# A row buffer that outlives its stage, and final stores cut into parts

## The chip, the cores and the metric

The kernel runs on one core of a Trainium2 chip. The metric is the device time of one launch in microseconds (us), shown as the median of several runs. Beside it stands one profiled execution, whose span, from the first to the last instruction, is a little shorter than the time of the same run. Engines: PE (TensorE), DVE (VectorE), ACT (ScalarE), POOL (GpSimd) and SP (SyncE, which here only issues DMAs).

## The reference

```python
# attention with random features, per batch (8) and head (8); q, k, v: 576 x 64; omega: 128 x 64
phi(x) = exp(h - max(h)) / sqrt(128),  h = x @ omega.T - |x|^2 / 2,  x scaled by 64**-0.25
attn   = (phi(q) @ (phi(k).T @ v)) / (phi(q) @ sum(phi(k)) + 1e-6)
x      = attn as (8, 576, 512)
# Fourier mixing, a norm and an MLP
u   = x + real(fft(fft(x, axis=1), axis=2))
un  = (u - mean(u)) / sqrt(var(u) + 1e-6)
out = u + relu(un @ w_ch1) @ w_ch2        # 512 -> 2048 -> 512, on 4608 rows
```

All is in 32-bit floats; the two MLP weights come in as 64-bit and are converted on the chip.

## The kernel before

The program has two parts. The first computes attention and mixing for all batches, writes `u` to a scratch tensor `us` in device memory, converts the weights, and already runs the MLP for the first 4 tiles of 128 rows (the "plain" blocks, `plain_of`, lines 862 to 923). The second part runs the MLP for the other 4096 rows in 8 blocks (`NTB`) of 512 rows, numbered j.

**The plain blocks.** Each multiplies by `w1` (L894), applies relu into `ht`, and multiplies by `w2` (L917) into a PSUM bank. `rest` (L925) loads the rows of `u` into a buffer `ur`, adds the bank (L930), and `store_rows` (L808) issues two stores of 64 rows (L810). `ur` is a tile with one buffer in the pool `mlpp`. This pool, `fix`, `ld`, `att` and `fft` are closed together by `early.close()` (L1066). The pool `late` (L1076) is opened after that and takes their room. Before all of them lie `const` and `slabs`, which live through both parts.

**A block of the second part.** Both matrix products use Strassen-like schemes of seven products.

- `first_of(j, fc)` (L1087) makes the hidden layer, for 8 values of `fc`. Its matmuls are L1099, each of the seven products 4 matmul records in the trace. Partial results are copied from PSUM into `s` by ACT (L1113) and added by DVE into `hid` (L1085); POOL forms sums `hs` (L1166). The weight sums `w1s` for groups 1 to 3 are written by DVE (L1045) at the start of the second part.
- `product_of(j, i, cells)` (L1193) makes one of seven products `i`, in the order 1, 2, 4, 5, 6, 7, 3 (`ORDER`), against weights that were prepared in device memory as `w2l`. Each product is split again into seven leaves (L1252, 8 matmul records each), which use operands loaded into a ring of tiles `wl` (L1182, `NWL` = 14 buffers, 256 KB a load), issued on SP's queue. The leaves run in the order 1, 2, 5, 6, 3, 7, 4. DVE adds bank and saved copy into quarters of `part` (c11, c12, c22; L1232); after the last leaf, ACT copies the fourth quarter, c21, from PSUM (L1282). `plus` (L1285) then adds `part` to a "cell" (L1289), on DVE or POOL.
- `second_of(j, cells)` (L1314) loads the rows of `u` of the block into two cells (tile `ur2`, each 128 partitions x 2 sets of 128 rows x 512 columns, shown as `ur` in the trace), and when all products that go into a cell are done it stores them, with four DMAs of 64 rows on SP (`stored`, L1322). A cell has a left and a right half of 256 columns (`HM`). The left half of cell 0 needs products 1 and 2; its right half needs 6, 5 and, last of all, 3. Cell 1 needs 4, 5, 6 and 7.

**What sets the order.** The order of the instructions on each engine is written by `Listing` (L82), a small planner that runs while the program is built: every piece of work is a `Step` with an engine, an assumed duration, the events and buffers that it waits for, and a bias; the step with the lowest sum of earliest begin and bias comes next, and takes its place on its engine. `port` marks steps of which only one may run on DVE and POOL together in the plan. The chip then runs each engine's list in order, with waits. SP's DMAs too are issued strictly in list order: a store that waits for its data holds up the loads behind it.

Of the kernel before, what the change touches and what calls it, by code (L numbers as in the profile page):

```python
# [14 lines left out]
ALU = mybir.AluOpType  # L15
AX = mybir.AxisListType
F32 = mybir.dt.float32
# [16 lines left out]
PE, ACT, DVE, POOL, SP, NONE = "pe", "act", "dve", "pool", "sp", "none"  # L34
# [192 lines left out]
def kernel(  # L227
# [10 lines left out]
    nc = tc.nc  # L238
# [3 lines left out]
    DM = H * D  # L242
# [10 lines left out]
    P = 128  # L253
# [9 lines left out]
    TP = 128  # L263
    NPLAIN = 4
    TB = 512
    NWL, NSUM = 14, 3
    NTB = (B * S - NPLAIN * TP) // TB
    HF, HT, HM = NFC // 2, TB // 2, DM // 2
    D2, F2 = NDC // 2, DFF // 2
# [6 lines left out]
    const = ctx.enter_context(tc.tile_pool(name="const", bufs=1))  # L276
# [2 lines left out]
    w1 = const.tile([128, NDC, DFF], F32, name="w1")  # L279

    slabs = ctx.enter_context(tc.tile_pool(name="slabs", bufs=4))
    ident = const.tile([128, 128], F32, name="ident")
    mhalf = const.tile([P, 1], F32, name="mhalf")

# [5 lines left out]
    mlpp = early.enter_context(tc.tile_pool(name="mlp", bufs=2))  # L290
# [495 lines left out]
    def rows_of(t):  # L786

        b, n = tiles[t]
        for i in range(2):
            h = slice(64 * i, 64 * i + 64)  # L790
            c, r = (b, n + i) if n else (b + i, 0)
            u0 = 64 * (n - 1 + i) if n else 2 * NL * P
            rows = out[c].rearrange("(p r) d -> r p d", r=R)[r]
            ev = ("us", c) if n > 4 else ("us", c, n // 2 if n else NL, 0)
            yield h, us[c][u0 : u0 + 64, :], rows, ev
# [4 lines left out]
    def load_rows(dst, t):  # L800
        b, n = tiles[t]
        if n:
            nc.sync.dma_start(dst, us[b][64 * (n - 1) : 64 * (n + 1), :])
        else:
            for h, u, _, _ in rows_of(t):
                nc.sync.dma_start(dst[h], u)

    def store_rows(t, src):  # L808
        for h, _, rows, _ in rows_of(t):
            nc.sync.dma_start(rows, src[h])  # L810

    unTs = {}

# [48 lines left out]
    def plain_of(j):  # L862
# [39 lines left out]
        for i in range(nt):  # L902
            for f0 in range(0, NFC, 2):
                yield Step(
                    PE,
                    1.72,
                    after=tuple(("ht", key, f) for f in (f0, f0 + 1))
                    + tuple(("w", NDC * DFF // CV + f) for f in (f0, f0 + 1)),
                    take=("bank",) if f0 == 0 else (),
                    give=("ht", "ht") if i == nt - 1 else (),  # L910
                    makes=("op", nt * j + i) if f0 == NFC - 2 else None, bias=0.24,
                )
                if f0 == 0:
                    b, yp = got()
                    yield Fork(rest(nt * j + i, b, yp))
                for fc in range(f0, f0 + 2):
                    nc.tensor.matmul(  # L917
                        yp[:, 0:DM],
                        lhsT=hs[fc][:, 128 * i : 128 * i + 128],
                        rhs=w2[:, fc, :],  # L920
                        start=(fc == 0),
                        stop=(fc == NFC - 1),
                    )

    def rest(t, b, yp):  # L925
        yield Step(SP, 0.5, 2.7, take=("ur",), kb=256)
        ur = mlpp.tile([P, DM], F32, name="ur", tag="ur", bufs=1)
        load_rows(ur[:], t)
        yield Step(DVE, 0.7, after=(("op", t),), give=(b,), bias=1.38)
        nc.vector.tensor_tensor(out=ur[:], in0=ur[:], in1=yp, op=ALU.add)  # L930
        yield Step(SP, 0.4, 2.5, give=("ur",), kb=256)
        store_rows(t, ur[:])
# [238 lines left out]
    ORDER = (1, 2, 4, 5, 6, 7, 3)  # L1171
# [13 lines left out]
    def factor(i):  # L1185

        g, t0 = {1: (0, 0), 2: (HF, 0), 4: (HF, HT), 7: (0, HT)}.get(i, (None, 0))
        if g is None:
            n = {5: 0, 6: 1, 3: 2}[i]
            return lambda t, f: hs[:, 4 * f : 4 * f + 4, n, 128 * t : 128 * t + 128]  # L1190
        return lambda t, f: hid[:, g + 4 * f : g + 4 * f + 4, t0 + 128 * t : t0 + 128 * t + 128]

    def product_of(j, i, cells):  # L1193
        a = factor(i)
        me = ("second", j, i)
        name = {1: "c11", 2: "c21", 4: "c22"}.get(i)

        def ready(*fq):
            fs = [f for q in fq for f in range(4 * q, 4 * q + 4)]
            return tuple((("first", j, f), name) if name else ("hs", j, f) for f in fs)  # L1200
# [3 lines left out]
        part = late.tile([128, 2, HM], F32, name="part", tag="part", bufs=4)  # L1204
# [34 lines left out]
        def leaf(n, ps, left, start, after=(), give=(), take=(), makes=None):  # L1239
            yield Step(  # L1240
                PE,
                0.895,
                after=(("wl", j, i, n),) + after,
                take=take,
                give=("wl",) + give,
                makes=makes, bias=0.3,
            )
            b = None
            if take:
                b, ps = got()  # L1250
            for f in range(4):
                nc.tensor.matmul(  # L1252
                    ps[:, 0:128],
                    lhsT=left[:, f],
                    rhs=wls[j, i, n][:, f],
                    start=start and f == 0,
                    stop=(f == 3),
                    skip_group_check=True,
                )
            return b, ps  # L1260

        def of_sum(n):
# [3 lines left out]
        xb, x = yield from leaf(1, None, a(0, 0), True, ready(0), take=one)  # L1266
# [11 lines left out]
        yield from leaf(  # L1278
            4, x, a(1, 1), False, ((me, "c22"),), give=("set", "sums"), makes=(me, "read")
        )  # L1280
        yield Step(ACT, 0.26, 0.1, give=(xb,), makes=(me, "c21"))
        nc.scalar.activation(out=part[:, 1, 0:128], in_=x[:, 0:128], func=AF.Copy)  # L1282
        yield Step(NONE, after=tuple((me, c) for c in ("c11", "c12", "c22")))
# [10 lines left out]
        def done(n):  # L1294
            return (("second", j, n), "done")

        us = tuple(("ur2", j, t) for t in range(2))
        if i in (1, 6, 7):
            if i != 1:
                before = {6: 1, 7: 6}[i]  # L1300
                yield from plus(cells["u"][:], part[:], after=(done(before),), give=("part",))
            to = {1: ((0, 0),), 6: ((0, 1),), 7: ((1, 1), (1, 0))}[i]
            part, give = cells["u"], ("part",) if i == 7 else ()
        else:
            to = {2: ((0, 0),), 4: ((1, 0),), 5: ((0, 1), (1, 1)), 3: ((0, 1),)}[i]
            give = ("part",)
        for n, (t, m) in enumerate(to):
# [3 lines left out]
                makes=done(i) if last else None,  # L1311
            )

    def second_of(j, cells):  # L1314
        t0 = (NPLAIN * TP + TB * j) // 128
        for t in range(2):
            yield Step(SP, 0.9, 3.0, take=("ur",), kb=512, makes=("ur2", j, t))
            cells[t] = late.tile([P, 2, DM], F32, name="ur2", tag="ur2", bufs=3)
            for n in range(2):
                load_rows(cells[t][:, n], t0 + 2 * t + n)  # L1320

        def stored(t, *after):  # L1322
            yield Step(
                SP, 0.9, 2.5, give=("ur",), after=tuple((("second", j, i), "done") for i in after),
                kb=512,
            )
            for n in range(2):
                store_rows(t0 + 2 * t + n, cells[t][:, n])

        yield Fork(stored(1, 4, 5, 7))  # L1330
        yield Fork(stored(0, 1, 2, 3, 5, 6))

        yield Step(
            NONE, after=tuple((("second", j, i), "read") for i in ORDER[:-1]), give=("ht",) * NFC
        )

    def halves():
        for j in range(NTB):
            for fc in range(HF):
                yield Step(NONE, take=("set", "ht", "ht"))  # L1340
                yield Fork(first_of(j, fc))
            cells = {}
            yield Fork(second_of(j, cells))
            for i in ORDER:
                yield Step(NONE, take=("set",))
                yield Fork(product_of(j, i, cells))
# [36 lines left out]
```

## Time and profile before

| | us |
|---|---|
| median of 3 runs | 1234.14 |
| lowest, highest | 1232.59, 1235.41 |
| profiled run: time | 1233.62 |
| profiled run: span | 1231.7 |
| second part, from its first matmul | about 468.5 to the end |
| last matmul's end | 1224.4 |

The profile's first part gives the busy time of each engine; its chain follows back from the last instruction to what released it, step by step. Beside the page, the trace answers questions: who waited for whom in a stretch of time, the chain in order of time, the busy time and granted TensorE clock of short stretches, and single instructions in order of time (start, duration, engine, line, what is written and read, how often, and in brackets how long the engine stood idle before and what released it). "SPq" stands for a DMA issued by SP, and its duration is the time that issuing takes; when the data has landed is told apart.

### The profile page before, as it was taken

The numbers are of one execution on the slowest core, as the hardware profiler recorded it, in microseconds if no ns is written. First come the engines' busy times: TensorE is split into PE (matmuls) and PEld (weight loads), VectorE is DVE, ScalarE is ACT, GpSimd is POOL, SyncE is SP. The second block draws the span as 40 slices with busy tenths as digits, with TensorE's granted clock in tenths as the row PEclk, the third lists the DMA queues.
The fourth block names the chain that finished last, engine by engine and source line by source line (L and its number), as shares of the span: only waits on it lengthen the run. The fifth ranks groups of instructions, "written<-read, shape, count | busy, mean of one in ns | idle before, by whom it ended". The sixth has DMA issues, their size and how long they took to land.

```text
span 1231.7 us, 31634 instructions
## 1 busy us (share of the span) xinstructions
PE 1192.3 (97%) x12705; PEld 1067.8 (87%) x12705; DVE 745.0 (60%) x1519; ACT 458.9 (37%) x1434; POOL 384.8 (31%) x451
## 2 busy tenths in 40 slices
PE   7889899999999999999999999999999999999997
PEld 6777878878878786899899899899899899899897
DVE  3888899887677643285185175276266266267255
ACT  6867768676664321222222222222222222222211
POOL 2353534532012012422431432431521431431421
PEclk9999999999999999999999999999999999999999
DMA  9564655636654324096186186276277277268255
GB/s 255 159 185 147 190 169 169 209 105 203 179 191 157 126 90 163 9 306 183 34 286 194 43 273 195 54 256 200 59 245 218 60 232 231 60 205 258 60 176 158
DMA packets 148737, 206.00 MB, mean 167 GB/s; under 512 B 49264, under 2 KB 62320, under 8 KB 148592
## 3 DMA queue, kind: packets, MB, share of 16 engines
q1 hardware_dynamic: 143984, 187.22, 49.4%
q0 software_dynamic: 4608, 16.78, 4.2%
q8 instruction: 100, 1.64, 0.5%
q14 instruction: 45, 0.37, 0.1%
HBM read 172.23 MB, written 35.91 MB: 169 GB/s over the span
## 4 chain that ended last, share of the span: by engine, by line
PE 91%; DVE 4%; ACT 2%; issue 1%; DMA 1%; SPq 0%; DVEq 0%; ACTq 0%
PE banks L1099 31%; PE banks L1252 29%; PE banks L515 5%; PE banks L917 5%; PE banks L894 4%; PE banks L441 4%; PE banks L683 4%; PE banks L549 3%; PE banks L592 2%; PE banks L710 2%; DVE nmx L459 2%; ACT e L476 1%; PE banks L833 1%; PE banks L715 1%; DVE raw L387 1%
## 5 line engine op out<-in xcount | busy, mean ns | idle before, releaser
L1085 DVE CUSTOM_DVE_ANT_0 hid<-banks,s 128x256 f32<-128x256 f32 x192 | 79.8, 423 | 256.3 <-PE banks L1099 256.3
L1252 PE MATMUL banks<-wl,sums 128*128 128x128 f32 x1792 | 220.3, 275 | 0.0
L1252 PEld LDWEIGHTS banks<-wl,sums 128*128 128x128 f32 x1792 | 210.5, 192 | 1.0
L476 ACT ACTIVATE e<-banks,nmx 128x128 f32<-128x128 f32 x576 | 160.1, 394 | 36.9 <-DVE nmx L459 36.8
L1113 ACT ACTIVATE s<-banks 128x256 f32<-128x256 f32 x192 | 73.4, 383 | 260.6 <-PE banks L1099 247.0
L1099 PE MATMUL banks<-unT,w 128*128 128x256 f32 x704 | 167.3, 379 | 0.0
L1099 PEld LDWEIGHTS banks<-unT,w 128*128 128x128 f32 x704 | 132.7, 190 | 17.9 <-issue 0.5
L1227 ACT ACTIVATE s<-banks 128x128 f32<-128x128 f32 x168 | 46.6, 277 | 236.5 <-PE banks L1252 174.6
L1099 PE MATMUL banks<-tt,w1s 128*128 128x256 f32 x512 | 127.4, 381 | 2.7 <-ACT s L1113 2.7
L459 DVE TENSOR_REDUCE nmx<-banks 128x8 f32<-128x1024 f32 (+1 forms) x96 | 88.3, 952 | 41.3 <-PE banks L515 36.7
L1099 PEld LDWEIGHTS banks<-tt,w1s 128*128 128x128 f32 x512 | 97.6, 191 | 16.4 <-ACT s L1113 3.1
L1166 POOL TENSOR_TENSOR hs<-hid 128x256 f32<-128x256 f32 x64 | 46.5, 726 | 202.7 <-DVE hid L1085 175.1
L1252 PE MATMUL banks<-wl,hid 128*128 128x128 f32 x768 | 98.8, 275 | 0.0
L1252 PEld LDWEIGHTS banks<-wl,hid 128*128 128x128 f32 x768 | 94.0, 192 | 1.2
L1232 DVE TENSOR_TENSOR part<-banks,s 128x128 f32<-128x128 f32 x168 | 48.6, 289 | 75.2 <-PE banks L1252 74.1
L1166 POOL TENSOR_TENSOR hs<-hid,hs 128x256 f32<-128x256 f32 x64 | 46.4, 726 | 118.5 <-issue 94.4
L515 PE MATMUL banks<-om,kqT 64*64 64x128 f32 x2304 | 78.0, 280 | 4.4 <-ACT kqT L448 3.0
L1099 PE MATMUL banks<-unT,w1s 128*128 128x256 f32 x320 | 81.5, 382 | 0.0
L827 POOL TENSOR_TENSOR rstd<-rstd,mhalf 128x1 f32<-128x1 f32 x36 | 29.8, 828 | 163.0 <-DVE rstd L825 163.0
L515 PEld LDWEIGHTS banks<-om,kqT 64*64 64x64 f32 x2304 | 65.2, 137 | 15.8 <-issue 4.7
L1252 PE MATMUL banks<-wl,hs 128*128 128x128 f32 x576 | 74.9, 275 | 0.4 <-DVE part L1232 0.4
L391 POOL TENSOR_TENSOR w<-w,raw 128x512 f32<-128x512 f32 x32 | 44.6, 1395 | 94.7 <-DVE raw L389 81.3
(110 smaller groups left out, 1997.0 us busy)
## 6 DMA issues: line engine op xcount, KB each, us to landing
wl<-w2l SPq DMA_DIRECT2D x392, 256.0 KB, 3.7
raw<-in_moe_w_ch_dram POOLq DMA_DIRECT2D x32, 512.0 KB, 5.2
kq<-in_k_dram SPq DMA_DIRECT2D x32, 288.0 KB, 3.7
kq<-in_q_dram SPq DMA_DIRECT2D x32, 288.0 KB, 4.1
vd<-in_v_dram SPq DMA_DIRECT2D x32, 288.0 KB, 4.7
out_dram<-ur SPq DMA_DIRECT2D x72, 128.0 KB, 2.4
u<-us SPq DMA_DIRECT2D x32, 256.0 KB, 4.2
ur<-us SPq DMA_DIRECT2D x32, 256.0 KB, 3.8
```

Of the source, the lines that this page charges most:

```text
L441: nc.tensor.transpose(ps[:, (j - j0) * 128 : (j - j0 + 1) * 128], src(j), ident[:])
L459: nc.vector.tensor_reduce(nmx[:, :, 0:num], pps[:, :, 0 : MF * num].rearrange("p b (c m) -> p b c m", m=MF), axis=AX.X, op=ALU.max, negate ...
L476: nc.scalar.activation(out=e[:, c + (i if num == 1 else 0), :], in_=pps[:, i, MF * c : MF * c + MF], func=AF.Exp, bias=nmx[:, i, c : c + 1],)
L515: nc.tensor.matmul(pps[cols, c, MF * m : MF * m + MF], lhsT=kqT[rows, j, cols], rhs=om2[rows, :],)
L683: nc.tensor.matmul(yp[:, 0:NK], lhsT=fold[:, c, n, :], rhs=tab[:, c, :], start=(c == 0), stop=(c == NC3 - 1),)
L894: nc.tensor.matmul(hp[:, 0:TP], lhsT=w1[:, dc, 128 * fc : 128 * fc + 128], rhs=unTs[key][:, dc, :], start=(dc == 0), stop=(dc == NDC - 1),)
L917: nc.tensor.matmul(yp[:, 0:DM], lhsT=hs[fc][:, 128 * i : 128 * i + 128], rhs=w2[:, fc, :], start=(fc == 0), stop=(fc == NFC - 1),)
L1085: nc.vector._custom_dve(TENSOR_ADD_SAT, out=o, in0=ps, in1=sb, s0=FMAX, s1=0.0)
L1099: nc.tensor.matmul(ps[:, 0:HT], lhsT=left(dc), rhs=right(dc), start=start and dc == 0, stop=(dc == D2 - 1), skip_group_check=True,)
L1113: nc.scalar.activation(out=s[:], in_=ps[:, 0:HT], func=AF.Copy)
L1166: nc.gpsimd.tensor_tensor(out=o, in0=l, in1=r, op=op)
L1252: nc.tensor.matmul(ps[:, 0:128], lhsT=left[:, f], rhs=wls[j, i, n][:, f], start=start and f == 0, stop=(f == 3), skip_group_check=True,)
```

## The change

There are three edits.

1. The row buffer of the plain blocks is no longer a tile of the pool `mlpp`, but a tile `ur1` of `const`, so that it keeps its place in the second part. It takes 2 KB of each partition, which the pool `late` then lacks; the ring `wl` gets 13 buffers instead of 14.
2. `store_rows` gets two more arguments, the columns to store and the queue for each half of the rows. In the last block the left half of cell 0 is stored after products 1 and 2. For the blocks before it the stores stay as they are. The assumed duration of `stored` in the planner goes from 0.9 to 2.4.
3. The last product (block 7, product 3) ends in a new function `ends`. For the first set of rows, once c11 and c12 are there, DVE adds them to the cell (128 x 256), and SP stores the right halves with two DMAs of 64 rows. For the second set of rows DVE adds c22 to the cell, and, after the last leaf, adds c21 straight from PSUM (128 x 128 each); then SP stores the first 64 rows and ACT the other 64. ACT's copy of c21 and the addition of the whole `part` to the cell are gone for this product.

```diff
-    NWL, NSUM = 14, 3
+    NWL, NSUM = 13, 3
...
     slabs = ctx.enter_context(tc.tile_pool(name="slabs", bufs=4))
+    ur1 = const.tile([128, DM], F32, name="ur1")
...
-    def store_rows(t, src):
-        for h, _, rows, _ in rows_of(t):
-            nc.sync.dma_start(rows, src[h])
+    def store_rows(t, src, cols=slice(None), queues=(nc.sync, nc.sync)):
+        for q, (h, _, rows, _) in zip(queues, rows_of(t)):
+            if q is not None:
+                q.dma_start(rows[:, cols], src[h])
...
-        ur = mlpp.tile([P, DM], F32, name="ur", tag="ur", bufs=1)
+        ur = ur1
...
+    def ends(j, me, part, x, cell):
+        t = (NPLAIN * TP + TB * j) // 128
+        before = tuple((("second", j, i), "done") for i in (5, 6))
+
+        def rows(n, e, queues, *after):
+            yield Step(e, 0.6, 2.5, after=after, kb=64)
+            store_rows(t + n, cell[:, n], slice(HM, DM), queues)
+
+        def first_rows():
+            yield Step(DVE, 0.42, after=((me, "c11"), (me, "c12")) + before, makes=(me, "r0"), port=True)
+            nc.vector.tensor_tensor(out=cell[:, 0], in0=cell[:, 0], in1=part[:, 0], op=ALU.add)
+            yield from rows(0, SP, (nc.sync, nc.sync), (me, "r0"))
+
+        yield Fork(first_rows())
+        for c, what, given in ((slice(128, 256), "c22", None), (slice(0, 128), "read", x)):
+            yield Step(DVE, 0.28, after=((me, what),) + before, makes=(me, "r1"), port=given is None)
+            nc.vector.tensor_tensor(
+                out=cell[:, 1, c],
+                in0=cell[:, 1, c],
+                in1=part[:, 1, c] if given is None else given[:, 0:128],
+                op=ALU.add,
+            )
+        yield Fork(rows(1, ACT, (None, nc.scalar), (me, "r1")))
+        yield from rows(1, SP, (nc.sync, None), (me, "r1"))
...
+        if (j, i) == (NTB - 1, ORDER[-1]):
+            yield from ends(j, me, part, x, cells[0][:, :, HM:DM])
+            return
...
-        def stored(t, *after):
+        def stored(t, cols, *after):
...
-                SP, 0.9, 2.5, give=("ur",), after=tuple((("second", j, i), "done") for i in after),
+                SP, 2.4, 2.5, give=("ur",), after=tuple((("second", j, i), "done") for i in after),
...
-                store_rows(t0 + 2 * t + n, cells[t][:, n])
-
-        yield Fork(stored(1, 4, 5, 7))
-        yield Fork(stored(0, 1, 2, 3, 5, 6))
+                store_rows(t0 + 2 * t + n, cells[t][:, n, cols], cols)
+
+        yield Fork(stored(1, slice(0, DM), 4, 5, 7))
+        if j < NTB - 1:
+            yield Fork(stored(0, slice(0, DM), 1, 2, 3, 5, 6))
+        else:
+
+            yield Fork(stored(0, slice(0, HM), 1, 2))
```

## The prediction

> **What bounds the kernel now.** I read the page first: the busy shares and the chain that ended last.
>
> ```profile
> span 1231.7 us, 31634 instructions
> PE 1192.3 (97%) x12705; PEld 1067.8 (87%) x12705; DVE 745.0 (60%) x1519; ACT 458.9 (37%) x1434; POOL 384.8 (31%) x451
> PE 91%; DVE 4%; ACT 2%; issue 1%; DMA 1%; SPq 0%; DVEq 0%; ACTq 0%
> ```
>
> TensorE (PE) is the bound almost everywhere, so a change can only pay where PE stands still or after its last matmul. Then I asked for the waits of PE alone from 460 us to the end, which is the whole second part:
>
> ```profile
> PE banks L1099 <- ACT s L1113: 2.7, 1, 2.7
> PE banks L1252 <- DVE part L1232: 0.4, 1, 0.4
> ```
>
> In 770 us PE waits twice. The long wait lies where the second part begins; the chain in order of time shows what it hangs on:
>
> ```profile
> 458.37 10.32 PE banks L917 x24
> ...
> 468.71 0.70 DVE ur L930
> ...
> 469.43 0.51 SPq L810
> ...
> 469.99 2.36 DMA out_dram<-ur
> ...
> 472.66 0.39 ACT s L1113
> 473.05 0.04 issue
> 473.09 9.08 PE banks L1099 x33
> ```
>
> The reader is to see that the first ScalarE (ACT) copy of the second part waits until the last plain block's row buffer `ur` has landed in the output; `ur` has nothing to do with `s`. The waits between 470 and 490 us name the same store for VectorE's (DVE) first write of `w1s`, another new tile, and SP's list names it for the first `wl` load. Three unrelated tiles wait for one buffer of 2 KB a partition: tiles of the pool `late` wait for everything that lived in the pools whose room they take, and `ur` is the last of it.
>
> Next, engines and clock in short stretches around the stall:
>
> ```profile
> 468.00:470.40 2.40, 2.40 (x10) 1.52 (x8) 0.69 (x1) 0.00 (x0) 0.00 (x0) 1.00 0.00 0
> 470.40:473.00 2.60, 0.00 (x0) 0.00 (x0) 0.56 (x1) 0.34 (x2) 0.00 (x0) 1.00 0.44 101
> 473.00:474.00 1.00, 0.91 (x2) 0.73 (x3) 0.97 (x3) 0.32 (x2) 0.00 (x0) 0.62 0.56 39
> 474.00:475.00 1.00, 1.00 (x4) 0.81 (x3) 1.00 (x3) 0.00 (x0) 0.00 (x0) 0.50 0.97 363
> 475.00:476.00 1.00, 1.00 (x4) 0.81 (x3) 0.96 (x3) 0.38 (x1) 0.00 (x0) 0.50 1.01 350
> 476.00:477.00 1.00, 1.00 (x4) 0.79 (x4) 1.00 (x3) 0.00 (x0) 0.00 (x0) 0.67 1.01 291
> ```
>
> The number behind the stretch is its length, then PE's busy time with its count; the third number from the end is the granted clock. The stall costs twice: PE is empty, and then runs at half clock to about 476.7 us.
>
> Last, the end of the program in order of time:
>
> ```profile
> 1222.86 0.29 DVE L1232 TENSOR_TENSOR part<-banks,s 128x128 f32<-128x128 f32 x1 [0.53 <-PE banks L1252]
> 1223.07 0.68 DVE L1289 TENSOR_TENSOR ur<-ur,part 128x512 f32<-128x512 f32 x1
> 1223.21 1.16 PE L1252 MATMUL banks<-wl,hs 128*128 128x128 f32 x8 [0.38 <-DVE part L1232]
> 1223.82 4.98 SPq L810 DMA_DIRECT2D out_dram<-ur  x8
> 1224.45 0.28 ACT L1282 ACTIVATE part<-banks 128x128 f32<-128x128 f32 x1 [3.10 <-PE banks L1252]
> 1224.77 0.69 DVE L1289 TENSOR_TENSOR ur<-ur,part 128x512 f32<-128x512 f32 x1 [1.01 <-ACT part L1282]
> ```
>
> The chain view ends at this DVE addition (1225.46), which misleads: SP issues eight stores back to back from 1223.82, four for the rows of cell 1 and four for cell 0, and is busy to 1228.80. All eight land 2.4 us after their issue, the early as the late, so they don't queue in the DMA engines; SP's issuing is the limit.
>
> [...] No ScalarE store is in this trace.
>
> **Part 1: `ur` moves into `const`.** The other last users of the early pools are the matmuls of L917 (`w2`, `ht`), over at 468.7. With `ur` gone from there, ACT's first copy needs only its own product. PE's product p1 runs 468.51 to 469.54; the copy takes 0.38 and ends near 469.95; p5 fills PE to 470.23 at its usual pace, so the next product finds its operand there. The next products, with the same copies, run from 477.48 without a wait.
>
> The saving is read from the start of the sixth product: before, it is at 477.48. A product is 4 matmul records, and 28 of them take 6.05 us at full clock (from the chain), 0.216 each. Without the stall five products from 468.51 end at 468.51 + 20 x 0.216 = 472.83. Difference 4.65 us: 2.69 of empty PE and about 1.9 of slow clock. From there PE has no wait but the 0.4 near the end, so all of it reaches the end.
>
> What could give it back: DVE's twelve weight sums (L1045) move from 472.44 to about 469.41, only 3.03 earlier, so DVE falls 1.6 us behind PE. Its three additions to `hid` end at 481.12 before, 478.09 after; the first product that needs one of them (`tt,w`) starts at 485.25 before, 480.60 after: 2.5 us to spare. SP's first `wl` load moves from 472.48 to about 470.6, behind the two stores; the first leaf needs it after 510 us. The reuse of one `ur` by four plain blocks waits for the same landings as before. Cost of these: nothing.
>
> **Part 2: ring `wl` of 13, not 14.** A load is issued when the leaf 14 places back has been read. In the last block's matmul stretch a leaf takes 0.87 us (8 records of 0.109) and a load lands in 3.3 to 4.5 us (5.5 at most in the run). With 13 it must land within 12 x 0.87 = 10.4 us. Nearly 5 us spare, and PE shows no wait for `wl` at all: nothing.
>
> **Part 3: the left half of cell 0 stored early.** Four stores after product 2, whose last addition is POOL's at 1196.42 to 1197.69. They take 4 x 0.62 = 2.5 us of SP among the `wl` loads and hold up those behind them by that, plus what SP waits for the addition (under 1 us: the written order and the addition both follow PE). Within the 5 us: nothing.
>
> **Part 4: the end.** Removed: ACT's copy (0.28), the 128x512 addition (0.69), and four of the eight closing stores. Added: `r0`, DVE 128x256; from the rows of 128 (0.29) and 512 (0.68) I interpolate 0.42 [...]; two 128x128 additions of 0.29, one reading PSUM, as L1232 already does; two stores of half rows, then one each from SP and ACT. `stored(1)` stays. The order is the listing's. Following its rule (earliest begin plus bias) with its own durations, DVE's order comes out as c22, `r0`, first `r1`, product 7's last addition, second `r1`; SP's as two stores of `r0`, four of cell 1, one of `r1`.
>
> On the clock of before: c22 at 1222.86; `r0` 1223.07 to 1223.49; first `r1` from 1223.41; product 7's addition 1223.62 to 1224.30 (0.55 later than now); second `r1` behind the last matmul, 1224.45 to 1224.74. SP: first store at 1223.56, then one per 0.627 (1223.82 to 1228.2 in seven steps); the third, cell 1's first, at 1224.81, when its data is ready; the seventh at 1223.56 + 6 x 0.627 = 1227.32. The last issue of before was at 1228.2: 0.9 us gained. ACT's store, issued near 1224.8, lands near 1227.2 and binds nothing.
> Bounds: half-row stores may be shorter (0.47 is the shortest issue of L810; three at 0.12 less) and land 0.2 sooner: gain up to 1.5, and 1.9 if `r0` comes ahead of c22. If the listing puts cell 1 first, SP starts at 1224.38 and ends its issues at 1228.14: no gain; a second queue to close may add 0.3 (estimate, like the closing steps of 0.3 each after 1230.6). I take 0.9, with -0.3 to 1.9.
>
> **Sum:** 4.65 + 0.9 = 5.55 us; span 1231.7 to 1226.15. The profiled run took 1233.62 against a span of 1231.7; the median is 1234.14. Taken from the median: 1228.6 us.
>
> **Rivals.**
> A (72%), the forecast: both parts work. 1228.6; own range 1226.3 to 1230.7. [...]
> B (13%): the stall goes, but its slow clock is not lost in the median run, or the end gives nothing: saving 2.7 to 4.65, so 1229.5 to 1231.4; I put it at 1230.5. [...] Against: the profiled run shows 0.50.
> C (8%): the change doesn't do its work at the start, because some other early buffer is released as late or new tiles wait for whole engines. Only the end gains: 1233.2. Against: ACT is released 0.01 us after the landing of `ur`'s store, and nothing else ends near.
> D (7%), slower: the ring of 13 starves PE. If a load's turn, from the freed buffer to use, reaches L, a leaf takes L/13. Up to 11.3 us (13 x 0.87) nothing happens. At 11.6, 0.023 x 392 leaves = 9 us are lost: 1228.6 + 9 = 1237.6, past 0.2% slower. For it: one leaf less of cover, and the early stores in SP's queue. Against: landings of at most 5.5 us, and no wait of PE.
>
> **How the numbers follow.** A measurement of this kernel can tell about 0.2% (2.5 us) from no change; the three times of before spread over 2.8. Faster: A and B, 85%. Same: C, 8%. Slower: D, 7%. The range leaves out C and D (15%) and a little of A's tails: 1226.2 to 1231.6.
>
> **What would show it.** Right: no PE wait on `s` near 470 us, the clock at 1.00 there, the `tt,w1s` products running on from 469.37; PE's last matmul near 1219.7; SP's last store about 2.9 us after PE's end; last ACT instruction a store. Wrong: PE idle near 470 for another releaser (C); PE or PEld waits naming `wl` (D); cell 1's stores first or SP idle between the closing stores (part 4); a PE wait on `hid` near 480 (part 1's give-back).

## The result, and the profile after

The changed kernel's median is 1228.55 us (1226.36 to 1230.91, 4 runs); its ratio to the kernel before is 0.9954, 95% interval 0.9931 to 0.9976. The forecast was 1228.6. The interval leaves out 1, so the gain is real, if small. The profiled execution of it has a span of 1228.9, more than the 1226.15 of the sum; where the difference lies is told below. The page's first lines and its chain:

```profile
span 1228.9 us, 31624 instructions
PE 91%; DVE 4%; ACT 3%; DMA 1%; issue 1%; SPq 0%; DVEq 0%; ACTq 0%
```

The waits of PE from 455 us to the end:

```profile
PE banks L1281 <- DMA wl<-w2l: 0.4, 1, 0.4
PE banks L1281 <- DVE part L1261: 0.4, 1, 0.4
```

The wait of 2.7 us is gone; a wait on the ring `wl` is new, which the prediction did not expect. (Lines have moved: L1102 is L1099 of before, L1281 is L1252, L1116 is L1113, L1261 is L1232, L1321 is L1289.) The same short stretches as before; the second part now begins at 470.46:

```profile
470.40:473.00 2.60, 2.60 (x13) 2.25 (x12) 2.31 (x4) 0.77 (x2) 0.00 (x0) 1.00 0.17 38
473.00:474.00 1.00, 1.00 (x6) 0.87 (x6) 1.00 (x3) 0.38 (x1) 0.00 (x0) 1.00 0.88 182
474.00:475.00 1.00, 1.00 (x7) 0.87 (x6) 0.96 (x2) 0.00 (x0) 0.00 (x0) 1.00 0.96 268
```

PE is busy throughout, and the clock stays at 1.00, in the later stretches up to 484 us too. The end, in order of time:

```profile
1220.81 0.29 DVE L1261 TENSOR_TENSOR part<-banks,s 128x128 f32<-128x128 f32 x1 [0.53 <-PE banks L1281]
1221.01 0.68 DVE L1321 TENSOR_TENSOR ur<-ur,part 128x512 f32<-128x512 f32 x1
1221.15 1.16 PE L1281 MATMUL banks<-wl,hs 128*128 128x128 f32 x8 [0.38 <-DVE part L1261]
1221.61 0.42 DVE L1207 TENSOR_TENSOR ur<-ur,part 128x256 f32<-128x256 f32 x1
1221.76 4.31 SPq L813 DMA_DIRECT2D out_dram<-ur  x7
1222.35 0.29 DVE L1213 TENSOR_TENSOR ur<-ur,banks 128x128 f32<-128x128 f32 x1
1222.66 0.56 ACTq L813 DMA_DIRECT2D out_dram<-ur  x1
```

SP issues seven stores instead of eight, and starts as long before PE's end (0.55 us) as it did before. In the order of DVE's additions product 7's last addition (L1321) still comes right behind c22, ahead of `r0` (L1207), so cell 1's stores are still the first.

Three stretches of an execution can be read from the timelines: up to the second part's first matmul; from there to PE's last matmul; from there to the span's end. All runs, the experiments told below included (us):

| run | first part | second part's matmuls | end | PE waits on `wl` |
|---|---|---|---|---|
| before | 468.51 | 755.86 | 7.33 | none |
| changed | 470.46 | 751.85 | 6.59 | 0.4 |
| ring 13 alone | 468.41 | 756.45 | 7.34 | 0.4 |
| `ur` in `const` alone (ring 13) | 467.85 | 751.24 | 7.31 | none |
| end alone | 471.75 | 755.81 | 6.54 | none |
| before with filler | 465.40 | 754.18 | 7.32 | none |
| changed, ring 12 | 467.31 | 761.77 | 6.62 | 6.0 |
| changed, loads in order of use | 468.08 | 751.19 | 6.53 | none |
| changed, two queues | 469.74 | 751.23 | 5.23 | none |
| changed, `r0` ahead | 466.77 | 751.20 | 5.93 | none |
| changed, three edits | 466.64 | 751.21 | 4.75 | none |
| changed, again | 469.67 | 751.21 | 6.52 | none |

The first column scatters by 6 us, though no edit changes the order of work there; the other two repeat to 0.1 us where nothing was edited, but for the wait on `wl`, which comes and goes. So a question of 1 us is put to the profile's stretches, and the timed ratios are the check.

### The profile page after: what moved, and what is told of

Its sections match the earlier page's. It is cut to its first block, busy times and chain, and to the rows that moved or that the text cites. A ratio compares the mean times of both kernels' runs of the same rounds, so it can differ in the third digit from the quotient of the medians.

```text
span 1228.9 us, 31624 instructions
## 1 busy us (share of the span) xinstructions
PE 1193.4 (97%) x12705; PEld 1068.7 (87%) x12705; DVE 745.9 (61%) x1521; ACT 458.5 (37%) x1433; POOL 385.4 (31%) x451
## 4 chain that ended last, share of the span: by engine, by line
PE 91%; DVE 4%; ACT 3%; DMA 1%; issue 1%; SPq 0%; DVEq 0%; ACTq 0%
PE banks L1102 31%; PE banks L1281 28%; PE banks L920 5%; PE banks L897 5%; PE banks L517 4%; PE banks L443 4%; PE banks L685 4%; PE banks L551 3%; PE banks L594 3%; ACT e L478 2%; PE banks L712 2%; PE banks L836 1%; DVE nmx L461 1%; PE banks L717 1%; PE banks L602 1%
## 5 line engine op out<-in xcount | busy, mean ns | idle before, releaser
L1281 PE MATMUL banks<-wl,sums 128*128 128x128 f32 x1792 | 220.2, 275 | 0.0
L1281 PEld LDWEIGHTS banks<-wl,sums 128*128 128x128 f32 x1792 | 210.5, 192 | 1.0
L1116 ACT ACTIVATE s<-banks 128x256 f32<-128x256 f32 x192 | 73.6, 383 | 255.8 <-PE banks L1102 255.8
L1102 PE MATMUL banks<-unT,w 128*128 128x256 f32 x704 | 167.3, 379 | 0.0
L1102 PEld LDWEIGHTS banks<-unT,w 128*128 128x128 f32 x704 | 132.7, 190 | 17.9 <-issue 0.5
L1102 PE MATMUL banks<-tt,w1s 128*128 128x256 f32 x512 | 126.3, 379 | 0.0
L1102 PEld LDWEIGHTS banks<-tt,w1s 128*128 128x128 f32 x512 | 97.3, 190 | 13.2
L1281 PE MATMUL banks<-wl,hid 128*128 128x128 f32 x768 | 98.9, 275 | 0.4 <-DMA wl<-w2l 0.4
L1281 PEld LDWEIGHTS banks<-wl,hid 128*128 128x128 f32 x768 | 94.0, 192 | 1.8 <-DMA wl<-w2l 0.6
L1261 DVE TENSOR_TENSOR part<-banks,s 128x128 f32<-128x128 f32 x168 | 48.6, 290 | 75.9 <-PE banks L1281 74.8
L1102 PE MATMUL banks<-unT,w1s 128*128 128x256 f32 x320 | 80.6, 379 | 0.0
L1281 PE MATMUL banks<-wl,hs 128*128 128x128 f32 x576 | 74.9, 275 | 0.4 <-DVE part L1261 0.4
```

The lines of the kernel that those rows point to most:

```text
L1102: nc.tensor.matmul(ps[:, 0:HT], lhsT=left(dc), rhs=right(dc), start=start and dc == 0, stop=(dc == D2 - 1), skip_group_check=True,)
L1116: nc.scalar.activation(out=s[:], in_=ps[:, 0:HT], func=AF.Copy)
L1281: nc.tensor.matmul(ps[:, 0:128], lhsT=left[:, f], rhs=wls[j, i, n][:, f], start=start and f == 0, stop=(f == 3), skip_group_check=True,)
```

## The experiments

**The ring alone.** Label e1_ring13.

```diff
-    NWL, NSUM = 14, 3
+    NWL, NSUM = 13, 3
```

> The kernel before with one edit: the ring wl has 13 buffers instead of 14; ur stays in the early pool and the end is as it was. My theory: a ring of 13 is at the edge, since leaves of three products are interleaved and the loads come in another order than they are used; the 15th load of a block is issued 5.4 us before its use and lands in up to 5.7 us. So 0 to 0.65 us of PE wait on wl in some of the 8 blocks, in all 0 to 2 us slower than before, and the 2.7 us stall near 470 us still there. Rival (my prediction as it was): the ring has 5 us to spare, no wait of PE on wl, ratio 1.000.

Measured: ratio 1.0006 (0.9992 to 1.002). The waits of PE from 400 us on:

```profile
PE banks L1099 <- ACT s L1113: 2.7, 1, 2.7
PE banks L1252 <- DMA wl<-w2l: 0.4, 1, 0.4
```

The stall is there, and one wait of PE on `wl`; the matmuls take 0.59 us more than before. The prediction's "nearly 5 us spare" is refuted; the price is small, too small for the timed ratio to show.

**The first part of the change alone.** Label e2_ur_const_only.

```diff
-    NWL, NSUM = 14, 3
+    NWL, NSUM = 13, 3
...
+    ur1 = const.tile([128, DM], F32, name="ur1")
...
-        ur = mlpp.tile([P, DM], F32, name="ur", tag="ur", bufs=1)
+        ur = ur1
```

> The change's first part alone: ur in const and the ring of 13, the end as in the kernel before. My theory: no PE wait near 470 us, clock 1.00 there, from the first matmul of the second part to PE's last one 751.2 to 751.9 us against 755.9 before (4.65 less for stall and slow clock, up to 0.65 given back to the ring); the end, from PE's last matmul to the span's end, 7.3 us as before. Time 4.0 to 4.7 us below before, ratio 0.9965. Rival 1: only the empty time counts, 2.7 us, ratio 0.998. Rival 2: the saving is the end's, ratio 1.000.

Measured: ratio 0.9961 (0.9949 to 0.9973). The matmuls take 751.24 against 755.86, that is 4.62 less; the end is unchanged. The `wl` wait doesn't occur in this execution. Both rivals are out: the saving is not the end's, and it is more than the 2.7 us of empty PE.

**The end alone.** Label e3_end_only: the changed kernel with these lines turned back.

```diff
-    NWL, NSUM = 13, 3
+    NWL, NSUM = 14, 3
...
-    ur1 = const.tile([128, DM], F32, name="ur1")
...
-        ur = ur1
+        ur = mlpp.tile([P, DM], F32, name="ur", tag="ur", bufs=1)
```

> The change's other part alone: ur back in the early pool, ring of 14, with the stores by parts and the final additions of the changed kernel. My theory: the stall near 470 us and the half clock after it are back; from PE's last matmul to the span's end 6.6 us against 7.3 before, because SP issues seven closing stores and not eight; time 0.7 us below before, ratio 0.9994. Rival 2: most of the 5.7 us comes from the end, ratio 0.996.

Its waits of PE from 400 us on:

```profile
PE banks L1100 <- ACT s L1114: 2.7, 1, 2.7
PE banks L1279 <- DVE part L1259: 0.4, 1, 0.4
```

The stall is back, and with it the half clock (0.56 and 0.58 in the two stretches of 2 us after it). The end is 6.54 against 7.33: 0.79 less, where 0.7 was expected. The timed ratio, 0.9983 (0.9973 to 0.9992), is 2.1 us and doesn't hold the 0.9994 that was expected; the profile shows nothing in the second part for the other 1.3 us, and the first part of this execution was the longest of all. That remainder stays open.

**Filling the stall.** Label e4_filler: matmuls that nothing reads stand where PE waits, so that only the emptiness of PE is taken away and not the wait.

```diff
         yield Fork(save("p5", z))
+        if j == 0 and fc == 0:
+            yield Step(PE, 2.6, take=("bank",))
+            fb, fill = got()
+            for n in range(6):
+                nc.tensor.matmul(fill[:, 0:HT], lhsT=w1[:, 0, f], rhs=un[0][:, 0])
+            yield Step(NONE, give=(fb,))
         yield Step(PE, mm, after=((me, "p1"),))
```

> The kernel before with six extra matmuls (128x128 by 128x256, 2.6 us at full clock, into a PSUM bank that nothing reads) placed on PE between the second and the third product of the second part, where PE stands still. Nothing else changes. My theory (the stall costs 2.7 us of empty PE and 1.9 us of half clock after it): the third product starts as before, 4.6 us after the first, but the clock stays at 1.00 and the sixth product starts about 7.2 us after the first instead of 9.0; time 1.8 us below before, ratio 0.9985, with more matmuls than before. Rival 1 (the slow matmuls after the stall have another cause, such as the wl loads that run at the same time): the sixth product starts 9 us after the first, ratio 1.000.

PE in order of time around the place (L1133 is the filler):

```profile
465.40 1.03 PE L1099 MATMUL banks<-unT,w 128*128 128x256 f32 x4
466.26 1.03 PE L1099 MATMUL banks<-tt,w1s 128*128 128x256 f32 x4
467.12 2.75 PE L1133 MATMUL banks<-unT,w 128*128 128x256 f32 x12
469.97 1.13 PE L1099 MATMUL banks<-tt,w1s 128*128 128x256 f32 x4
470.94 1.89 PE L1099 MATMUL banks<-unT,w1s 128*128 128x256 f32 x8
472.67 1.89 PE L1099 MATMUL banks<-unT,w 128*128 128x256 f32 x8
```

The third product starts 4.57 us after the first, as before (4.58), since it waits for the same store; but the sixth starts at 7.27 and not at 8.97, and the clock is 1.00 in every stretch of 2 us from 468 to 480. Six useless matmuls save 1.7 us in the profile (755.86 to 754.18), and the timed ratio is 0.9987 (0.9979 to 0.9994). The `wl` loads run beside these matmuls as before (DMA share 0.82 to 1.05 from 470 to 480 us), so they don't make them slow; it is the half clock that follows the idle PE.

**A ring of 12.** Label e5_ring12: the list is planned for 13 buffers, so every engine's order is kept, and the chip gets 12.

```diff
-                    wl = late.tile([128, 4, 128], F32, name="wl", tag="wl", bufs=NWL)
+                    wl = late.tile([128, 4, 128], F32, name="wl", tag="wl", bufs=NWL - 1)
```

> The changed kernel with a ring wl of 12 buffers, the order of every engine kept as it is with 13. My theory (leaves are used in another order than they are loaded, so with 13 the 15th and 16th load of a block have only 4 and 6 leaves of 0.89 us between the leaf that frees their buffer and their use): with one buffer less they have 3 and 5, 2.7 and 4.5 us, against landings of 2.7 to 5.7, so PE waits for wl in nearly every block, 1 to 3 us a block over 7 or 8 blocks, 8 to 20 us slower than the changed kernel: 1236 to 1248. Rival (my prediction as it was, cover of nearly the whole ring; the one wait of 0.4 us was chance): no more than that one wait, 1228 to 1230.

```profile
PE banks L1281 <- DMA wl<-w2l: 6.0, 12, 1.3
```

Twelve waits; ratio 1.005 (1.0034 to 1.0067), and 10.5 us more of matmul stretch than with 13 and no wait, as the theory had it. The loss is more than the 6.0 us listed: with 13 a wait listed at 0.4 cost 0.64, and twelve such differences are 3 of the 4.5 us between; the rest is open. Nor is it the landing alone: in the first block SP issues three loads of rows of `u`, from 518.90 to 520.65, ahead of a `wl` load whose buffer, by the count of leaves, is free by then. One buffer less turns the change into a loss: 13 is the last size that mostly holds.

**Loads in the order of use.** Label e6_order_of_use. In PE's list leaves of up to three products are interleaved: the loads of a block, numbered from 0 as they are issued, are used in the order 0, 7, 1, 8, 2, 9, 14, 3, 10, 15 and so on. Load 14 is the seventh to be used.

```diff
+    USE = (0, 7, 1, 8, 2, 9, 14, 3, 10, 15, 4, 11, 16, 5, 12, 17, 6, 13, 18, 19, 21, 22, 20, 23, 24, 28, 25, 29, 26,
+           30, 35, 27, 31, 36, 32, 37, 33, 38, 34, 39, 42, 40, 43, 41, 44, 45, 46, 47, 48)
...
-            for i in ORDER:
-                for n, l in enumerate(PARTS):
+            for k in USE:
+                for i, (n, l) in ((ORDER[k // 7], (k % 7, PARTS[k % 7])),):
```

> The changed kernel with one edit: the wl loads of a block are issued in the order in which PE uses them, instead of product by product. PE's order is the same. My theory: with 13 buffers every load then has at least 9 leaves (8 us) of cover, no PE wait on wl, 0 to 0.65 us less than the changed kernel: from the second part's first matmul to PE's last one 751.2 us. Rival: loads are limited by something else (bandwidth at the start of a block's matmul stretch, where rows of u are loaded too), and the wait of 0.4 us comes again.

Measured: no wait on `wl`, 751.19 us of matmuls, ratio 0.9959 (0.9943 to 0.9974). It does what was expected, but four of the six executions with 13 buffers in the old order had no wait either, so this execution, and the one of the three edits below, don't show that the wait is gone for good.

**The closing stores on two queues.** Label e7_two_queues. Products 4, 5 and 7 release cell 1's stores, now one step on SP and one on ACT; the stores of `r0` are split likewise.

```diff
-            yield from rows(0, SP, (nc.sync, nc.sync), (me, "r0"))
+            yield Fork(rows(0, ACT, (None, nc.scalar), (me, "r0")))
+            yield from rows(0, SP, (nc.sync, None), (me, "r0"))
...
-        yield Fork(stored(1, slice(0, DM), 4, 5, 7))
+        if j < NTB - 1:
+            yield Fork(stored(1, slice(0, DM), 4, 5, 7))
+        else:
+            yield Fork(shared(SP, (nc.sync, None), ("ur",)))
+            yield Fork(shared(ACT, (None, nc.scalar), ()))
```

> The changed kernel with one edit: at the end each pair of closing stores is split, the first 64 rows on SP, the other 64 on ACT (4 issues each instead of 7 and 1). My theory (SP's issuing is the limit at the end): SP's last issue comes 3 x 0.62 = 1.9 us sooner, and from PE's last matmul to the span's end 4.7 us instead of 6.6; ratio to the changed kernel 0.9985. Rival (the DMA engines are the limit, and 768 KB at the 205 GB/s seen there take 3.7 us whatever queue issues them): stores land later after their issue and 0 to 0.5 us are gained.

```profile
1220.43 2.68 ACTq L813 DMA_DIRECT2D out_dram<-ur  x4
...
1220.42 2.40 SPq L813 DMA_DIRECT2D out_dram<-ur  x4
```

The end is 5.23: of 1.9 us expected 1.3 to 1.4 came, more than the rival's 0.5. Both queues issue at once, at the old pace on SP (0.60 a store) and at 0.67 on ACT, and the one landing that the profile gives is 2.5 us. The DMA engines were no limit at the old pace: with one queue they are busy for 0.95 of the stretch from 1223 to 1224 us of the changed kernel and move 207 GB/s, but with two queues the same 768 KB were through 1.3 to 1.4 us sooner after PE's end. Issuing is the larger limit, and ACT is the slower of the two (2.68 us for its four stores against 2.40). The ratio to the kernel before is 0.9955 (0.9938 to 0.9971).

**`r0` ahead.** Label e9_r0_ahead. In the change, `ends` is reached only after the step of the last leaf has been placed; product 7's addition has its place by then. Here `first_rows` is forked before leaf 7, after which c22 is formed, with a bias of -1.5 and without the `port` mark. The text below says that the prediction took this order for granted; in fact it had c22 first and `r0` second, and named `r0` ahead of c22 only as its best case, worth 1.9 us. This run is that best case; the order of the stores on SP is the forecast one.

```diff
-            yield Step(DVE, 0.42, after=((me, "c11"), (me, "c12")) + before, makes=(me, "r0"), port=True)
+            yield Step(DVE, 0.42, after=((me, "c11"), (me, "c12")) + before, makes=(me, "r0"), bias=-1.5)
...
+        if (j, i) == (NTB - 1, ORDER[-1]):
+            yield from ends(j, me, part, x, cells[0][:, :, HM:DM], True)
         yield from leaf(7, x, s3, False, of_sum(7) + ((me, "u2"),))
...
```

> The changed kernel with the order that my prediction took for granted: the first addition of the last product (r0, 128x256) stands ahead of c22 in DVE's order, and its two stores ahead of cell 1's in SP's. My theory: r0 fits into DVE's idle time before c22, SP's first closing store is issued about 1 us sooner, and the seven issues end 0.9 us sooner; from PE's last matmul to the span's end 5.7 us instead of 6.6. Rival: DVE's r0 delays c22, and with it PE's last leaf and cell 1, by what it gains.

```profile
1215.96 0.45 DVE L1207 TENSOR_TENSOR ur<-ur,part 128x256 f32<-128x256 f32 x1
1216.46 0.29 DVE L1263 TENSOR_TENSOR part<-banks,s 128x128 f32<-128x128 f32 x1
1216.67 0.68 DVE L1325 TENSOR_TENSOR ur<-ur,part 128x512 f32<-128x512 f32 x1
...
1216.43 4.67 SPq L813 DMA_DIRECT2D out_dram<-ur  x7
```

`r0` fits in front of c22 (L1263), PE's wait before the last leaf stays at 0.38, and SP's first store is issued 1.54 us ahead of PE's end instead of 0.55. The end is 5.93 against 6.59; 0.66 of the expected 0.9, since the seven issues took SP 4.67 us there and not 4.31. Ratio 0.9952 (0.9933 to 0.997).

**The three edits together, and the change again.** Labels e8_three_edits and e10_change_again, on one chip.

> The changed kernel with the three edits of the runs before together: wl loads in the order of use, r0 ahead of c22, closing stores shared by SP and ACT. My theory: no wait of PE on wl (751.2 us from the second part's first matmul to PE's last one), and from PE's last matmul to the span's end 4.6 us: the last store waits for the addition of c21 (about 0.35 after PE's end), is issued behind cell 1's two on each queue at about PE's end + 0.9, takes 2.5 to land and 1.1 to close. About 2 us below the changed kernel, 6.5 to 7 below before, ratio to before 0.9945. Rival (two queues take ScalarE's and SP's issues longer, 0.67 each, as in the run with two queues): 5.2 us from PE's end, as there.

> The changed kernel as it is, on the same chip. My theory: no stall near the start of the second part and clock 1.00 there; from the second part's first matmul to PE's last one 751.2 us, or up to 0.65 more where a wl load lands late (one execution of two so far); 6.6 us from there to the end; ratio to before 0.996. Rival: the wl wait is fixed at one place and comes in every execution, 751.85.

The three edits: 1225.69 us, ratio 0.9951 (0.9935 to 0.9967), matmuls 751.21, end 4.75, nearer the theory's 4.6 than the rival's 5.2. The change again: 1228.19 us, ratio 0.9972 (0.9959 to 0.9985), 751.21 and 6.52, with no wait on `wl`, so that wait is not fixed at one place. In the profile the three edits take 1.77 us off the end of the change; in the timed medians the distance is 2.5 us, with intervals that overlap. By the ratios of its two measurements the change is worth 3.5 to 5.7 us. Its first part alone was timed at 0.9961, between the two, so the timed ratios don't show the end's 0.8 us; only the profile does.

## Why the prediction was right, point by point

- **The stall (part 1).** Forecast 4.65 us, of it 2.69 of empty PE and about 1.9 of half clock. Measured 4.62 with the first part of the change alone, 4.65 in the second execution of the change. The filler shows 1.7 us of it to be the clock. By starts of products, 0.864 us apart at full clock, the third was 2.85 us late and the clock cost 1.8; the 2.69 is counted from the modelled end of a matmul. That `ur` held the new tiles is shown by moving it: with that part alone PE has no wait there, and in the changed kernel the first ACT copy (471.57), the first `w1s` (471.26) and the first `wl` load (472.70, 0.18 after its store's issue) no longer wait for that store to land. That a tile of `late` waits for everything in the closed pools, and not only for what lay in its own bytes, is inferred from three tiles waiting for one buffer of 2 KB; no run put it to the test. DVE's lag behind PE cost nothing, as worked out: no wait of PE on `hid` is listed.
- **The ring (part 2): the step that failed.** I took the cover of a load as nearly the whole ring, "12 x 0.87 = 10.4 us". That holds only if leaves are used in the order of their loads. In PE's list they are not. The second leaf of a block frees the buffer of load 14 and the third that of load 15; between that and the use load 14 has 4 leaves and load 15 has 6, or 3.6 and 5.3 us at 0.89 a leaf. In the chain of the changed kernel load 15, issued at 803.77 as soon as the third leaf was over, lands at 809.45:

```profile
803.77 5.67 DMA wl<-w2l
```

  Its leaf was due at 808.94; it starts at 809.49 and takes 1.16 us instead of 1.06. The term was set at nothing and measured 0.64 us (751.85 against 751.21 in the second execution), in one of the two executions of the change; the run with the ring alone lists a wait on `wl` of 0.4 us too. Why load 15 landed so late is open. Rival D named the right mechanism, with a threshold of 11.3 us that was twice too high; the run with 12 buffers shows how close it was.
- **The early left half (part 3).** No new wait of PE in the last block: nothing, as forecast.
- **The end (part 4).** Forecast 0.9, measured 0.74 to 0.81. The size is nearly right, the order behind it was not: I had `r0` and its stores ahead of cell 1, and product 7's addition delayed by 0.55. The list has product 7's addition first, and what is saved is one issue of SP's eight. For cell 1's stores first, which is what came, I had written no gain, because I still delayed that addition; so the near hit of this term is in part luck. My best case, `r0` ahead of c22, I put at 1.9; that run gives 1.4 against before. And "all eight land 2.4 us after their issue" read too much: the trace of before holds a landing for one of the eight only, the third (2.37), so it doesn't show whether the others queued. That issuing was the limit is shown by the run with two queues, whose end is 1.3 to 1.4 us shorter.
- **The span.** 1228.9 is 2.75 above the sum: 1.95 from a longer first part in this execution (470.46 against 468.51), 0.64 from the ring, 0.16 from the end. The median hit the forecast more closely than the terms deserve: the base of 1234.14 was a median of three runs, and later medians of before lie between 1231.38 and 1232.58; the second median of the change is only 3.8 us below the one of before beside it. That the first one agreed to 0.05 us is luck; the stretches, which save 4.75 and 5.46 us against 5.55 forecast, are the fair comparison.
- **Rivals.** B and C are out in the profile: the half clock was there in all three executions that have the stall unfilled, and in none of the others, where products start about 0.86 us apart; the stall went with `ur`. That a median execution might not lose the slow clock was the author's estimate; none of the three was without it. Two of the signs that the prediction named for being wrong were there all the same: a PE wait naming `wl`, and cell 1's stores first.

## What to carry to other kernels

When a pool is opened in the room of closed ones, look at which last instruction of the old pools its first tiles wait for; one small buffer that is stored late can hold up several engines (here ACT, DVE, SP and, through ACT, PE by 2.85 us), and a half TensorE clock after the gap, here 1.7 to 1.8 us on top of 2.85, makes it dearer. The cover of a prefetch ring is counted on the consumer's own order, leaf by leaf (here 3.6 us for load 14, not 10.4), not from the number of buffers. At the end of a program count the DMA issues behind the last matmul: here which queue issued how many set the end, more than the arithmetic did (in the changed kernel DVE's last addition is over at 1222.64, and SP issues until 1226.07).

## What the runs showed of the hardware

A PE gap of 2.69 to 2.70 us was followed by half clock in three of three executions: the granted clock was 0.50 in before and in the run with the ring alone, 0.56 and 0.58 over stretches of 2 us with the end alone. In the one where the gap was filled it stayed at 1.00. In the first part the clock dips in all four executions that were read there, at places that differ: in stretches of 30 us from 30 to 150 us the mean clock of before was 1.00, 0.94, 1.00, 1.00, of the changed kernel 0.94, 0.89, 1.00, 0.94, of the end alone the same, and of before with filler 1.00, 0.90, 0.99, 1.00. In the changed kernel PE stood still before these dips too: the half clock begins at about 34.4, 75.3 and 140.2 us, 1 to 2 us after gaps of 1.45, 2.01 and 1.53 us ended. But gaps of 1.50, 1.81 and 1.87 us in the same execution were followed by none, so the length of a gap alone doesn't decide. Of these four executions the two with the longest first parts (470.46 and 471.75 us) have the most half clock from 30 to 150 us, but the shortest (465.40) has more there than before (468.51); how much of the scatter the dips explain was not tried.
